# One step for the second batch's numerators, with its attention, the down products and the first output weights moved earlier

## The chip, the core and the metric

The kernel runs on one core of a Trainium2 chip. TensorE (PE) multiplies matrices, VectorE (DVE), ScalarE (ACT) and GpSimd (POOL) do elementwise work, and SyncE (SP) issues most DMA transfers. Each engine runs its instructions in the order in which the program gives them, and engines wait for each other by semaphores. The metric is the device time of one execution in microseconds (us). Before the change it is 306.09 us, the median of three runs (305.92 to 306.23).

## The reference

```
phi(x) = outer(S1 @ x, S2 @ x)            # 8 x 8 = 64 features for each token and head
kv  = sum over s of phi(k)[s] v[s]        # 64 x 32 for each batch and head
z   = sum over s of phi(k)[s]
x   = (phi(q) @ kv) / (phi(q) @ z + 1e-6) # the attention's output
x   = x as rows: 4352 tokens x 128        # 4 batches x 1088 tokens, 4 heads x 32
out = (silu(x @ w_gate) * (x @ w_val)) @ w_out   # 128 -> 1536 -> 128
```

The inputs are float64 in memory; the kernel reads them as pairs of 32-bit words. The attention needs all keys of a batch before the first output of that batch exists. The feed-forward part is three products of 4352 x 128 x 1536.

## The kernel before, in words

**Units and down products.** The tokens are cut into 12 blocks, three to a batch: two of 384 tokens and one of 320. The 1536 hidden columns are cut into 12 chunks of 128. `unit(i, j)` makes block i's chunk j: two PE products (gate and val, L773) into two PSUM banks, Silu of the gate on ACT (L779), and gate times val on DVE (L790) into one of 27 slots of `hbuf`. `down()` takes the first entry of `todo` and multiplies that chunk by `wo[:, j, :]`, adding into the block's bank (L804). After chunk 11, `store` transposes the block on DVE (L833) and SP writes it out (L839). The first six units are `late`: DVE is busy then, so ACT copies the val product and POOL multiplies later (`catch_up`, L796).

**Banks.** `bank()` hands out four PSUM banks in turn (g0, g1, g2, acc); once down products begin, `free_banks.pop()` takes `acc` out of the turn for the sums. Block 1's sum lies in g1, every other block's in acc (`down`).

**Weights.** The float64 weights arrive in pieces: gate and val in five (chunks 0, 1-2, 3-5, 6-8, 9-11), `wo` in four of three chunks each, `("wo", 0)` to `("wo", 3)`. `load_next` takes the next piece from the list `coming` and loads it into one of four raw buffers (L152). `narrow` turns a piece into float32 in three steps, each `part(name, i)` taking one: two DVE operations on the high words (L216, L217); two ACT operations (L221, L222); two DVE operations (L224, L230) and the final product (L239, on POOL but for the first val piece and half of each two-chunk piece, which DVE does), after which the next piece's load is issued. For the first val piece alone (`split`), the third step is cut in two, so that L224 is issued ahead of the first block's division results (L486) and the rest behind them.

**The loop around the change.** After a startup that mixes batch 0's attention, the first weight pieces and six late units, a loop runs over `seq`, 30 units of batch 0 numbered z = 0 to 29. z = 12 to 14 are block 0's chunks 6 to 8, z = 15 to 17 block 1's, z = 18 to 20 block 2's (320 tokens); z = 21 to 29 are chunks 9 to 11 in the same way. `parts` says after which unit a step of a later weight piece is issued: a piece's steps stand at z, z+1 and a little later. From z = 17 on each unit is followed by one `down()` (in the order block 0 chunk 0, 1, 2, ...) and by one step of `attentions()`. The rest of batch 0's down products follow the loop without units between them. Then batches 1 to 3 run as 36 units each, with a down product after each unit.

**The attention of batches 1 to 3** is the generator `attentions()`; each `yield` ends a step. For batch 1: transposes of k and q (L274, L509), key products and query sketches on PE (L301, L289), key features on DVE (L324), their sums on POOL (`feature_sums`, L494), key-value sums on PE (`values`, L335, L638), a copy and a transpose of them (`spread_out`, L648, L652) and six DMAs that spread them over the partitions (L658, L659). Then `query_step` on DVE: query features against the key sums (L679), reduction (L686), a reciprocal and a scaling (L695 to L701), features again (L324) and their transpose (L710). Last, `numerators` on PE (L730) and copies to `xT` (L747), from which batch 1's units read. Before, batch 1's query step and numerators run in two parts: the first three of nine column groups ahead of batch 1's first unit (up to the mark `"first"`), the other six while block 3 (batch 1's first) is worked on.

Of the kernel before, what the change touches and what calls it, by code (L numbers as in the profile page):

```python
# [18 lines left out]
def kernel(  # L19
# [28 lines left out]
    nc = tc.nc  # L48
    P = nc.NUM_PARTITIONS
# [6 lines left out]
    NC = (NX + 3) // 4  # L56
    F = R * R
    NCH = Dff // P
# [45 lines left out]
    wv = const.tile([P, NCH, P], FP32, name="wv")  # L104
# [6 lines left out]
    raw = {}  # L111
# [23 lines left out]
    coming = [(w, i) for i in range(len(pieces["wg"])) for w in ("wg", "wv")]  # L135
    coming += [("wo", i) for i in range(len(pieces["wo"]))]

    def load_next():
        if not coming:
            return  # L140
        name, i = coming.pop(0)
        dst, src = weights[name]
        c0, c1 = pieces[name][i]
        if name == "wo":
            part = src.rearrange("(c p) d -> p c d", p=P)[:, c0:c1, :]
        else:
            part = src.rearrange("p (c f) -> p c f", f=P)[:, c0:c1, :]
        if not wide_w:
            nc.sync.dma_start(out=dst[:, c0:c1, :], in_=part)
            return  # L150
        t = raw[name, i] = stage.tile([P, 3, P], I64, tag="raw", name="raw", bufs=NRAW)
        nc.sync.dma_start(out=t[:, 0 : c1 - c0, :], in_=part)  # L152
# [42 lines left out]
                ps[0:32, 0:w], warm[:, 0:32], warm[:, 0:w], start=True, stop=True  # L195
            )

    def narrow(dst, raw, shape, engine=nc.gpsimd, split=False):

        words = raw.bitcast(I32)
        pat = "p (n w) -> p n w" if len(shape) == 2 else "p c (n w) -> p c n w"
        words = words.rearrange(pat, w=2)
        lo = words[..., 0].bitcast(U32)
        hi = words[..., 1]
        first = len(shape) == 2  # L210
        tag = "s" if first else ""
        e, m = (
            stage.tile(shape, I32, tag=n + tag, name=n, bufs=6) for n in ("exp", "man")
        )
        f = m[:].bitcast(FP32)
        nc.vector.tensor_scalar(e[:], hi, 0x7FF00000, None, op0=ALU.bitwise_and)  # L216
        nc.vector.tensor_scalar(  # L217
            m[:], hi, 0xFFFFF, 0x100000, op0=ALU.bitwise_and, op1=ALU.bitwise_or
        )
        yield  # L220
        nc.scalar.activation(e[:], e[:], AF.Relu, bias=rebias[: shape[0], :], scale=8.0)  # L221
        nc.scalar.activation(f, m[:], AF.Copy, scale=2.0**-20)  # L222
        yield
        nc.vector.scalar_tensor_tensor(  # L224
            out=e[:], in0=hi, scalar=-(1 << 31), in1=e[:],
            op0=ALU.bitwise_and, op1=ALU.bitwise_or,
        )
        if split:
            yield
        nc.vector.scalar_tensor_tensor(  # L230
            out=f, in0=lo, scalar=2.0**-52, in1=f, op0=ALU.mult, op1=ALU.add
        )
        mul = nc.vector if first else engine
        p2 = e[:].bitcast(FP32)
        todo = [(mul, slice(None))]
        if shape[1] == 2:
            todo = [(nc.vector, slice(0, 1)), (mul, slice(1, 2))]
        for engine, c in todo:
            engine.tensor_tensor(out=dst[:, c], in0=f[:, c], in1=p2[:, c], op=ALU.mult)  # L239
        if not first:  # L240
            load_next()
        yield

    def narrow_w(name, i):
        c0, c1 = pieces[name][i]
        if wide_w:
            dst = weights[name][0]
            t = raw.pop((name, i))
            split = (name, i) == ("wv", 0)
            engine = nc.vector if split else nc.gpsimd  # L250
            yield from narrow(
                dst[:, c0:c1, :], t[:, 0 : c1 - c0, :], [P, c1 - c0, P], engine, split
            )

    def run(*gens):
        for g in gens:
# [200 lines left out]
    def divide(b, x0, n, nd, among=()):  # L457


        w = 32 * n  # L460
        t0 = S * b + 64 * x0
        dT = apool.tile([P, 2 * XS, 32], FP32, tag="dT", name="dT", bufs=2)
        rc = apool.tile([P, 2 * XS], FP32, tag="rc", name="rc", bufs=2)
        rd = apool.tile([P, 2 * XS, 32], FP32, tag="rd", name="rd", bufs=2)
        nc.vector.transpose(
            out=dT[:, 0 : 2 * n, :].rearrange("p (a x) t -> p a x t", a=2),
            in_=nd[1][:, :, 0:w].rearrange("p a (x t) -> p a x t", t=32),
        )
        for name in among[:1]:
            part(name, 0)  # L470
        nc.vector.tensor_scalar_add(rc[:, 0 : 2 * n], dT[:, 0 : 2 * n, 0], 1e-6)
        nc.vector.reciprocal(rc[:, 0 : 2 * n], rc[:, 0 : 2 * n])
        nc.vector.transpose(
            out=rd[:, 0 : 2 * n, :], in_=rc[:, 0 : 2 * n].unsqueeze(2).to_broadcast([P, 2 * n, 32])
        )
        for name in among[1:]:
            part(name, 0)
        xs = xT[:, t0 : t0 + 2 * w].rearrange("p (x a t) -> p a x t", a=2, t=32)
        rs = rd[:, 0 : 2 * n, :].rearrange("p (a x) t -> p a x t", a=2)
        flat, deep = "p (x t) -> p x t", "p a (x t) -> p a x t"  # L480
        if isinstance(nd[0], list):
            todo = [(xs[:, a], nd[0][a][:, 0:w].rearrange(flat, t=32), rs[:, a]) for a in (0, 1)]
        else:
            todo = [(xs, nd[0][:, :, 0:w].rearrange(deep, t=32), rs)]
        for x, num, r in todo:
            nc.vector.tensor_tensor(out=x, in0=num, in1=r, op=ALU.mult)  # L486
        for name in among[1:]:
            part(name, 0)
# [43 lines left out]
    def attentions():  # L532
# [15 lines left out]
        fac = None, qab  # L548
# [28 lines left out]
            (NC - 1, NC, kvz[:, 1, 0 : 2 * F], kvz[:, 1, 2 * F : 4 * F]),  # L577
        ])
        spread = spread_out(1, kvz[:, 0, :])
        for _ in range(4):  # L580
            yield
            run_copies(copies, 1)
        step = query_step(1, fac, spread)
        yield from step(0, 3)
        numerators(1, spread, 0, 3)
        yield "first"
        yield from step(3, NC)
        phk = hbuf[:, NH - 6 :, :].rearrange("p s (n h i j) -> p (s n) h i j", h=1, i=R, j=R)
        phk = phk.rearrange("p (c h) o i j -> p c (h o) i j", h=H)
        yield from features(phk, fac2, ())  # L590
        zs = feature_sums(phk)
        yield from turns(3)
        yield "pe"
        numerators(1, spread, 3, NC)
        kv = bank()
        values(kv, phk, zs)
        kp, qp = wide("a"), wide("b")
# [21 lines left out]
    def run_copies(copies, n):  # L619
        for f, *args in copies[:n]:  # L620
            f(*args)
        del copies[:n]
# [175 lines left out]
    def down():  # L798

        i, j = todo.pop(0)  # L800
        n = SPLIT if i == LAST else blocks[i][1]
        if j == 0:
            acc[i] = bank("g1" if i == 1 else "acc")
        nc.tensor.matmul(  # L804
            acc[i][:, 0:n],
            wo[:, j, :],
            hidden[i, j][:, 0:n],
            start=(j == 0),
            stop=(j == NCH - 1),
        )  # L810
        if i != LAST:
            hidden.pop((i, j))
            slots.append(slot_of[i, j])
        if j == NCH - 1:
            store(i, n)
# [34 lines left out]
    def part(name, i):  # L850

        next(fills[name, i], None)
# [96 lines left out]
    def parts_of(n):  # L949

        for _ in range(n):
            if ahead[0] not in ("pe", "end"):
                ahead[0] = next(att, "end")
# [34 lines left out]
    def both(i, *names):  # L988
        return [(name, i) for name in names]
# [1 line left out]
    w = ("wg", "wv")  # L991

    parts = {}
    for z, p in enumerate(both(3, *w) + both(4, *w) + [("wo", i) for i in range(4)]):
        z += z // 2 * 4
        for at in (z, z + 1, z + 2 + z % 6):
            parts.setdefault(at, []).append(p)
# [2 lines left out]
    seq += [(i, j) for j0 in (6, 9) for i in range(3) for j in range(j0, j0 + 3)]  # L1000
    order = [(i, j) for i in range(3) for j in range(NCH)]
    for z, (i, j) in enumerate(seq):
        if z == 17:
            free_banks.pop()
            turn[0] %= 4
        unit(i, j)
        for p in parts.get(z, ()):
            part(*p)
        if z in (24, 25, 26):
            catch_up()  # L1010
        if z == 6:
            load_k(1)
            load_v(1, [nc.sync] * 4)
            load_q(1)
        if z >= 17:
            todo.remove(order[0])
            todo.insert(0, order.pop(0))
            down()
        if z >= 17:
            parts_of(1)  # L1020
    todo.sort()
    while todo:
        for _ in range(min(3, len(todo))):
            down()
        if ahead[0] != "first":
            parts_of(1)
    while ahead[0] != "first":
        parts_of(1)

    slots[:] = range(NH - 6)  # L1030

# [2 lines left out]
    for b in range(1, B):  # L1034
        for z in range(3 * NCH):
            i, j = z // NCH, z % NCH
            if (b, z) in ((1, NCH), (2, 0), (2, 2 * NCH)):
                group()
            unit(3 * b + ((0, 2, 1)[i] if b == B - 1 else i), j)
            for _ in range(2):  # L1040
                if len(todo) > LAG:
                    down()
            parts_of(2 if b == 1 and z in (0, 4, 6, 7, 8) else 1)
    ps = wide("a")[:, 0, 0:D]
    for j in range(NCH):
        if todo and j % 4 == 0:
# [40 lines left out]
```

## Time and profile before

| what | value |
|---|---|
| median of the runs | 306.09 us (305.92 to 306.23) |
| the profiled execution: its own time | 306.09 us |
| its span in the trace | 304.4 us |
| PE busy | 297.9 us, 2186 matmul records |
| DVE busy | 170.0 us |
| ACT busy | 93.8 us |
| POOL busy | 37.8 us |
| granted PE clock | 1.00 throughout |

The time around the span is 306.09 - 304.4 = 1.7 us. A float32 product shows up as two matmul records. Ends of matmuls are modelled and overlap their successor, so the starts tell how long a product holds PE: in a run of 384-token products they are 0.645 us apart, in a run of 320-token products 0.54 us. A row of the timeline gives start, duration, engine, line and operation, then the tiles written and read; a bracket at its end gives the idle time of the engine before it and what ended that.

### The profile page before, as it was taken

Reading aid. Unit: us, or ns where it says so; the run is one execution under the profiler, and the core shown is the slowest. Engines: PE = TensorE matmul, PEld = TensorE weight load, DVE = VectorE, ACT = ScalarE, POOL = GpSimd, SP = SyncE. Lnnn points to the kernel's source line nnn. Section 1 sums busy time; section 2 is a strip of 40 time slices with the busy share of each in tenths; the row PEclk is TensorE's granted clock in tenths of the full one; section 3 lists DMA queues with packets and bytes.
Section 4 is the critical chain, followed back from the end, with each engine's and each line's share of the span. In section 5 each row is a group of like instructions: output and inputs, shape, how many; then the busy total and the mean of one; then the engine's idle time right before and its main releaser. Section 6 shows DMA issues by size and latency. Waiting matters only on the chain.

```text
span 304.4 us, 5416 instructions
## 1 busy us (share of the span) xinstructions
PE 297.9 (98%) x2186; PEld 190.4 (63%) x2186; DVE 170.0 (56%) x334; ACT 93.8 (31%) x219; POOL 37.8 (12%) x54
## 2 busy tenths in 40 slices
PE   8899999999999999999999999999999999999995
PEld 7545566657665557555676655555676556676664
DVE  3997988692636991788932478822323322333321
ACT  3566764422102222322222222222322222222230
POOL 3216222174000051070000000000000000000000
PEclk9999999999999999999999999999999999999999
DMA  7463390404511000400100200100100100100101
GB/s 197 139 201 106 103 313 12 149 14 146 117 28 22 0 2 20 110 0 0 26 3 2 49 0 2 26 0 0 22 6 0 22 3 0 26 0 2 21 0 26
DMA packets 26136, 14.57 MB, mean 48 GB/s; under 512 B 18688, under 2 KB 24192, under 8 KB 26112
## 3 DMA queue, kind: packets, MB, share of 16 engines
q1 hardware_dynamic: 25456, 14.13, 18.1%
q8 instruction: 17, 0.28, 0.3%
q10 hardware_dynamic: 656, 0.10, 0.2%
q14 instruction: 7, 0.06, 0.1%
HBM read 11.41 MB, written 2.23 MB: 45 GB/s over the span
## 4 chain that ended last, share of the span: by engine, by line
PE 95%; DVE 2%; DMA 2%; issue 0%; ACT 0%; SPq 0%
PE bank L773 58%; PE bank L804 28%; DMA kld<-in_k_dram 2%; PE a L730 1%; PE b L289 1%; PE bank L335 1%; PE a L819 1%; PE a L301 1%; PE bank L348 0%; PE bank L301 0%; PE a L392 0%; PE a L444 0%; PE a L335 0%; PE b L301 0%; PE b L730 0%
## 5 line engine op out<-in xcount | busy, mean ns | idle before, releaser
L790 DVE TENSOR_TENSOR hbuf<-sg,bank 128x384 f32<-128x384 f32 (+1 forms) x138 | 72.9, 529 | 99.3 <-PE bank L773 97.6
L779 ACT ACTIVATE sg<-bank 128x384 f32<-128x384 f32 (+1 forms) x144 | 68.0, 473 | 163.0 <-PE bank L773 159.8
L773 PE MATMUL bank<-xT,wg 128*128 128x384 f32 (+1 forms) x288 | 112.5, 472 | 0.0
L773 PE MATMUL bank<-xT,wv 128*128 128x384 f32 (+1 forms) x288 | 111.5, 469 | 0.2 <-DVE wv L239 0.2
L804 PE MATMUL bank<-hbuf,wo 128*128 128x384 f32 (+2 forms) x288 | 105.1, 460 | 0.0
L773 PEld LDWEIGHTS bank<-xT,wv 128*128 128x128 f32 x288 | 54.5, 190 | 33.7 <-DVE hbuf L790 0.9
L804 PEld LDWEIGHTS bank<-hbuf,wo 128*128 128x128 f32 x288 | 54.5, 190 | 32.0
L773 PEld LDWEIGHTS bank<-xT,wg 128*128 128x128 f32 x288 | 53.7, 190 | 32.3 <-issue 1.6
L494 POOL TENSOR_TENSOR zs<-hbuf 128x1024 f32<-128x1024 f32 x2 | 4.7, 2360 | 51.5 <-DVE hbuf L324 37.6
L833 DVE STREAM_TRANSPOSE o<-bank 128x384 f32<-128x384 f32 (+2 forms) x12 | 6.6, 549 | 7.8 <-PE bank L804 7.5
L679 DVE TENSOR_TENSOR phq<-spread,qab 128x768 f32<-128x768 f32 x9 | 9.7, 1076 | 0.5 <-DMA spread<-spread 0.5
L221 ACT ACTIVATE exp<-exp,rebias 128x384 int32<-128x384 int32 (+3 forms) x15 | 8.3, 551 | 2.3 <-DVE exp L216 1.7
L710 DVE STREAM_TRANSPOSE phT<-phq 128x768 f32<-128x768 f32 x9 | 8.7, 968 | 0.1
L686 DVE TENSOR_REDUCE dot<-phq 128x96 f32<-128x768 f32 x9 | 8.5, 947 | 0.1
L324 DVE TENSOR_TENSOR phq<-qab 128x768 f32<-128x768 f32 x9 | 8.5, 942 | 0.0
L747 ACT COPY xT<-a 128x64 f32<-128x64 f32 (+3 forms) x7 | 2.3, 367 | 18.2 <-PE b L730 11.8
L224 DVE SCALAR_TENSOR_TENSOR exp<-raw,exp 128x384 int32<-128x384 int32 (+2 forms) x14 | 7.0, 503 | 0.0
L230 DVE SCALAR_TENSOR_TENSOR man<-raw,man 128x384 f32<-128x384 uint32 (+2 forms) x14 | 6.9, 492 | 0.0
L222 ACT ACTIVATE man<-man 128x384 f32<-128x384 int32 (+3 forms) x15 | 6.8, 452 | 0.0
L494 POOL TENSOR_TENSOR zs<-zs 128x512 f32<-128x512 f32 (+1 forms) x6 | 6.6, 1100 | 0.5
L239 POOL TENSOR_TENSOR wg<-man,exp 128x384 f32<-128x384 f32 (+1 forms) x5 | 4.0, 801 | 18.2 <-DVE man L230 14.0
L274 DVE STREAM_TRANSPOSE kT<-kld 128x384 f32<-128x384 f32 (+2 forms) x9 | 5.9, 690 | 0.6 <-DMA kld<-in_k_dram 0.6
(127 smaller groups left out, 161.4 us busy)
## 6 DMA issues: line engine op xcount, KB each, us to landing
kld<-in_k_dram SPq DMA_DIRECT2D x4, 544.0 KB, 4.6
vld<-in_v_dram SPq DMA_DIRECT2D x12, 144.0 KB, 5.3
qld<-in_q_dram SPq DMA_DIRECT2D x3, 544.0 KB, 4.4
raw<-in_moe_w_out_dram SPq DMA_DIRECT2D x4, 384.0 KB, 4.5
out_dram<-o SPq DMA_DIRECT2D x28, 48.0 KB, 1.8
raw<-in_moe_w_gate_dram SPq DMA_DIRECT2D x3, 384.0 KB, 3.4
raw<-in_moe_w_val_dram SPq DMA_DIRECT2D x3, 384.0 KB, 3.7
out_dram<-o SPq DMA_DIRECT2D x16, 40.0 KB, 1.7
```

What stands on the lines that cost most here:

```text
L221: nc.scalar.activation(e[:], e[:], AF.Relu, bias=rebias[: shape[0], :], scale=8.0)
L224: nc.vector.scalar_tensor_tensor(out=e[:], in0=hi, scalar=-(1 << 31), in1=e[:], op0=ALU.bitwise_and, op1=ALU.bitwise_or,)
L230: nc.vector.scalar_tensor_tensor(out=f, in0=lo, scalar=2.0**-52, in1=f, op0=ALU.mult, op1=ALU.add)
L324: engine.tensor_tensor(out=phk[:, c0:c1, :, :, :].rearrange("p c h i j -> p (c h) i j"), in0=ka.unsqueeze(3).to_broadcast([P, n, R, R]), i ...
L494: add = lambda o, a, b: nc.gpsimd.tensor_tensor(out=o, in0=a, in1=b, op=ALU.add)
L679: nc.vector.tensor_tensor(out=phq[:, c0:c1, :, :, :], in0=zrep.unsqueeze(1).to_broadcast([P, n, H, R, R]), in1=f.unsqueeze(3).to_broadcast ...
L686: nc.vector.tensor_reduce(out=dot[:, x, :], in_=phq[:, c0:c1, :, :, :].rearrange("p c h j i -> p (c h) j i"), axis=AX.X, op=ALU.add,)
L710: nc.vector.transpose(out=phT[:, :, :, c0:c1, :].rearrange("p h g c t -> p c (h g) t"), in_=phq[:, c0:c1, :, :, :].rearrange("p c h (g i) ...
L773: nc.tensor.matmul(o[:, 0:n], w[:, j, :], xT[:, t0 : t0 + n], start=True, stop=True)
L779: nc.scalar.activation(sg[:, 0:n], g[:, 0:n], AF.Silu)
L790: nc.vector.tensor_tensor(out=hj[:, 0:n], in0=sg[:, 0:n], in1=u[:, 0:n], op=ALU.mult)
L804: nc.tensor.matmul(acc[i][:, 0:n], wo[:, j, :], hidden[i, j][:, 0:n], start=(j == 0), stop=(j == NCH - 1),)
```

## The change

It does six things. The query step and the numerators of batch 1 are done in one piece of nine column groups, ahead of batch 1's first unit. The attention generator is advanced from z = 13 on instead of 17. Down products follow the units from z = 14 instead of 17 (up to z = 25, and one after z = 29), the bank `acc` leaves the turn at z = 14, and the load of batch 1's k, v and q is asked for after z = 5 instead of 6. After the loop the numerators are issued when four down products are left. The load and the narrowing of `("wo", 0)` move ahead of the last gate and val pieces. The cut in the first val piece's third step goes away, so that its L224 comes behind the division results.

```diff
     coming = [(w, i) for i in range(len(pieces["wg"])) for w in ("wg", "wv")]
     coming += [("wo", i) for i in range(len(pieces["wo"]))]
+    coming.remove(("wo", 0))
+    coming.insert(-5, ("wo", 0))
...
-        if split:
-            yield
         nc.vector.scalar_tensor_tensor(
             out=f, in0=lo, scalar=2.0**-52, in1=f, op0=ALU.mult, op1=ALU.add
         )
...
-        for name in among[1:]:
-            part(name, 0)
         xs = xT[:, t0 : t0 + 2 * w].rearrange("p (x a t) -> p a x t", a=2, t=32)
...
-        for _ in range(4):
+        for _ in range(2):
             yield
-            run_copies(copies, 1)
-        step = query_step(1, fac, spread)
-        yield from step(0, 3)
-        numerators(1, spread, 0, 3)
+            run_copies(copies, 2)
+        yield from query_step(1, fac, spread)(0, NC)
         yield "first"
-        yield from step(3, NC)
+        numerators(1, spread, 0, NC)
+        yield
...
         yield "pe"
-        numerators(1, spread, 3, NC)
         kv = bank()
...
-    for z, p in enumerate(both(3, *w) + both(4, *w) + [("wo", i) for i in range(4)]):
+    late = both(3, *w) + [("wo", 0)] + both(4, *w) + [("wo", i) for i in range(1, 4)]
+    for z, p in enumerate(late):
         z += z // 2 * 4
         for at in (z, z + 1, z + 2 + z % 6):
             parts.setdefault(at, []).append(p)
...
-        if z == 17:
+        if z == 14:
             free_banks.pop()
             turn[0] %= 4
         unit(i, j)
         for p in parts.get(z, ()):
             part(*p)
         if z in (24, 25, 26):
             catch_up()
-        if z == 6:
+        if z == 5:
             load_k(1)
             load_v(1, [nc.sync] * 4)
             load_q(1)
-        if z >= 17:
+        if 14 <= z < 14 + NCH or z == len(seq) - 1:
             todo.remove(order[0])
             todo.insert(0, order.pop(0))
             down()
-        if z >= 17:
+        if z >= 13:
             parts_of(1)
     todo.sort()
     while todo:
-        for _ in range(min(3, len(todo))):
+        for _ in range(min(3, len(todo) - 4)):
             down()
-        if ahead[0] != "first":
-            parts_of(1)
+        for _ in range(2):
+            if ahead[0] != "first":
+                parts_of(1)
+        if len(todo) == 4:
+            break
     while ahead[0] != "first":
         parts_of(1)
+    parts_of(1)
+    while todo:
+        down()
...
-            parts_of(2 if b == 1 and z in (0, 4, 6, 7, 8) else 1)
+            parts_of(1)
```

The narrowing steps therefore stand as follows (loop index z after whose unit each of the three steps is issued):

| piece | before | after |
|---|---|---|
| wo 0 | 12, 13, 14 | 6, 7, 8 |
| wg 4, wv 4 | 6, 7, 8 and 7, 8, 10 | 7, 8, 10 and 12, 13, 14 |
| wo 1 | 13, 14, 16 | 13, 14, 16 |
| wo 2 | 18, 19, 20 | 18, 19, 20 |
| wo 3 | 19, 20, 22 | 19, 20, 22 |

| first down product that reads the piece | before | after |
|---|---|---|
| wo 0 (chunk 0) | z = 17 | z = 14 |
| wo 1 (chunk 3) | z = 20 | z = 17 |
| wo 2 (chunk 6) | z = 23 | z = 20 |
| wo 3 (chunk 9) | z = 26 | z = 23 |

More of the change, by code (lines that the diff above doesn't have):

```diff
@@ L196, in keep_warm, with narrow @@
             )
-    def narrow(dst, raw, shape, engine=nc.gpsimd, split=False):
+    def narrow(dst, raw, shape, engine=nc.gpsimd):
         words = raw.bitcast(I32)
@@ L248, in narrow_w @@
             t = raw.pop((name, i))
[L249 to L253, printed above, removed]
+            engine = nc.vector if (name, i) == ("wv", 0) else nc.gpsimd
+            yield from narrow(dst[:, c0:c1, :], t[:, 0 : c1 - c0, :], [P, c1 - c0, P], engine)
     def run(*gens):
```

## The prediction

> **What bounds the kernel now.** I read the page's busy shares and clock first, then PE's waits, then the timelines of PE, DVE and POOL from 44 to 120 us.
>
> ```profile
> PE 297.9 (98%) x2186; PEld 190.4 (63%) x2186; DVE 170.0 (56%) x334; ACT 93.8 (31%) x219; POOL 37.8 (12%) x54
> ...
> PEclk9999999999999999999999999999999999999999
> ```
> ```profile
> engine line waited for: us in total, times, longest us
> PE bank L194 <- PEq L1071: 0.9, 1, 0.9
> ...
> PE bank L773 <- DVE wv L239: 0.2, 1, 0.2
> ```
>
> PE is the bound. It is full at full clock; its waits are short and lie in the startup, and from 27 us on product follows product. So the change can gain only what it takes off PE, and loses whatever makes PE stand still. The rows I price with:
>
> ```profile
> 53.86 0.70 PE L773 MATMUL bank<-xT,wv 128*128 128x320 f32 x2
> ...
> 72.66 0.29 PE L289 MATMUL a<-s,qT 128*32 128x64 f32 x8
> ...
> 90.00 2.96 PE L804 MATMUL bank<-hbuf,wo 128*128 128x320 f32 x10
> ...
> 116.07 1.21 PE L335 MATMUL bank<-hbuf,vld 128*32 128x64 f32 x72
> ...
> 164.69 1.21 PE L335 MATMUL bank<-hbuf,vld 128*32 128x64 f32 x72
> ```
> ```profile
> 54.67 0.49 DVE L790 TENSOR_TENSOR hbuf<-sg,bank 128x320 f32<-128x320 f32 x1
> 55.07 0.55 DVE L224 SCALAR_TENSOR_TENSOR exp<-raw,exp 128x384 int32<-128x384 int32 x1
> 55.54 0.55 DVE L230 SCALAR_TENSOR_TENSOR man<-raw,man 128x384 f32<-128x384 uint32 x1
> ...
> 78.77 0.96 DVE L679 TENSOR_TENSOR phq<-spread,qab 128x768 f32<-128x768 f32 x1 [0.50 <-DMA spread<-spread]
> ```
> ```profile
> 56.17 1.00 POOL L239 TENSOR_TENSOR wo<-man,exp 128x384 f32<-128x384 f32 x1 [5.39 <-DVE man L230]
> ```
>
> The reader is to see wo 2's last step: unit z = 20 starts its val product at 53.86, DVE multiplies it 0.81 later, then come L224, L230 and POOL's product, and the weights are ready at 57.17, 3.31 us after 53.86. Today the first down product that reads them starts at 62.74, so nobody notices.
>
> **The change part by part.** Times are on before's clock; products hold PE 0.645 us (384) or 0.54 (320).
>
> *Numerators, a gain.* The first part fills the time between the down products (a run from 77.50; 12 x 0.645 + 7 x 0.54 later it is 89.02) and the next down product at 90.00: 0.98. The second lies between a down product of 114.15 (+ 0.645) and the value sums at 116.07: 1.27. One full set, batch 2's, lies between a down product of 162.56 (+ 0.54) and 164.69: 1.59. So 2.25 become 1.59: **-0.66**. The small DVE operations of the query step also become fewer, hidden behind PE.
>
> *The bitwise sum, a loss.* L224 of the first val piece runs at 14.44, before the division product at 14.74, which waits for PE's product of 14.09 + 0.56. It lies in DVE idle time today. Behind it, it lengthens a DVE chain without gaps up to the val weights that end PE's wait at 19.02. Its price is the spacing L224 to L230 of that size (13.10 to 13.27): **+0.17**. Ends: 0 (some gap absorbs it) and 0.28 (a whole operation).
>
> *Loads.* The wo 0 load takes the slot of 23.52 in SP's queue, the last gate and val pieces slide one slot each to 26.18 and 33.33. They land within 6.2 us (the longest landing of such a piece), by 32.4 and 39.5, for first steps that run after 37 and at 43.5. Batch 1's k is issued at about 35.7, as now, and lands within 6.1, by 41.8; its transpose now runs at 45.4. q, by 38.13 + 7.0 = 45.1, is read at 48.6. v, four transfers from 36.24, is read at 67.7. Cost 0; each us that k came later than 45.4 would hold unit 14's product behind it on DVE. No more is issued than before. Attention's ACT copies lie in ACT's gaps of 1.44 us per unit, at cost 0.
>
> *wo 1, a wait.* Units 14 to 16, now with a down product each, start 1.94 us apart: 44.07, 46.01, 47.94. Unit 17 starts at 49.88, its down product (chunk 3, from wo 1) is due at 51.17. Unit 16's val product starts at 48.59, DVE multiplies at +0.91 = 49.50, L224 at 49.98, L230 at 50.45, POOL 0.63 later, 51.08 to 52.08. POOL to PE is not timed before; the nearest row is DVE to PE, 0.15 (val weights end 18.87, PE 19.02). PE resumes at 52.23: **+1.07**. Ends 0.9 and 1.3 (half to a whole L224 of delay either way).
>
> *wo 2, a wait.* From 52.23: key products and sketches follow as today 0.74 and 2.34 later, unit 18 at 55.31, unit 20's val product at 59.39, its down product (chunk 6, from wo 2) due at 59.93. Unit 20's DVE product could start at 59.39 + 0.81 = 60.20, but key features are queued before it (unit 18's product 56.76, two weight operations 0.27 each, features 2 x 0.60, unit 19's 58.90, the same with one feature operation) and it starts at 60.44. L224 0.40 later, L230 another 0.47, POOL another 0.63, 1.00 of product, 0.15: PE resumes at 63.09. **+3.15**. Ends 2.9 (DVE free) and 3.5. Behind the waiting down product stands everything on PE; ACT and DVE then wait for PE.
>
> The Trainium skill ("TensorE: Matmul & The Clock Gate", Part 1) says that a PE left idle for a whole window of about 3.4 us falls to half clock, until it has been busy for about such a window. That speaks against this change, since the wait above comes near it. No idle stretch in this trace is above 0.9 us and no slice shows less than full clock, so no row here tests it. By the page the sum would be an estimated 1.7 us more (half of 3.4); I leave it out.
>
> wo 3 is not late: on POOL it now follows the feature sums (from 62.9; 5.3 us as 64.91 to 70.23 before) and its own L230 at 68.2, is ready at 69.8, and its reader is due at 72.7. The feature sums themselves end 68.2; their reader (L638) is due at 68.7. Thin: each us late there is a us on PE.
>
> *The query step among the units, a wait.* From 63.09 PE runs a down product (0.645) and units 21 and 22 with one each (1.94 apiece), then the value sums 0.09 later at 67.7; the last sketches start 3.38 after these (69.28 to 72.66 before) at 71.07, unit 23's val product at 72.03 and unit 25's at 75.91. From last sketches to L679 it takes 78.77 - 72.66 = 6.11 us (copy, transpose, six DMAs issued one after another), so L679 starts at 77.18. Before, nothing urgent was queued behind it. Now unit 25's DVE product is, due at 76.82 and run at 78.05. Then DVE alternates: product 0.47 or 0.40, store transpose 0.51, L679 or L686 0.87 (spacings at 85.44 to 85.95 and 97.14 to 98.47). Unit 26 gets 79.90, 27 81.24, 28 82.51, 29 83.78. Units from 26 on have no down products between them, so three banks run out: block 1's sum takes g1, which unit 29's val product (30 units after z = 14 on a turn of three) has just filled. It must wait for DVE: 83.78 + 0.49 + 0.13 = 84.40, against 81.73 if nothing waited: **+2.67**. Ends 0.8 (only the delay of unit 25) and 3.6 (another DVE operation of 0.95 in the way).
>
> After that DVE has 12 us of down products for its remaining 7 us of query step, and the numerators find their input ready; block 3 starts 2.2 us after them, more than the 0.6 us of copies.
>
> **Sum**: -0.66 + 0.17 + 1.07 + 3.15 + 2.67 = +6.40. The profiled execution took 306.09 us (span 304.4, 1.7 around it), the same as the median: 312.5.
>
> **Rivals.**
> 1. *Only the weights stall.* The banks or an earlier spread hide the last wait: 306.09 + 3.73 = 309.8. For: DVE idles for 3.9 and 1.2 us near this place before. Against: L679 is tied to the sketches on PE, whatever else moves.
> 2. *The attention is later still*: a queue or sum that I hold for thinly covered (feature sums 0.5 us, spread DMAs) slips, and PE restarts slowly after standing still. Bounded by one more spread of 1.9 us (a transfer's landing): 314.4.
> 3. *The other side: the weights are in time.* If PE doesn't wait for wo 1 and wo 2 (their POOL products done by 51.0 and 59.8, over 3 us sooner than I work out), DVE's backlog must also vanish; then only the gain and the bitwise sum are left, 305.6. Against: the instruction order has wo 2's last step behind unit 20's DVE product, and PE's product behind that on a wait for POOL; both are dependences of data.
> 4. *The change does less than it says*: the numerators are still two sets in effect. The order shows one set of 32 products on PE, so no weight.
>
> **How the numbers follow.** My forecast 0.67, rival 1 0.17, rival 2 0.11, rival 3 0.05. The time is the forecast's, 312.5. Its own ends: the low ends sum to -0.66 + 0 + 0.9 + 2.9 + 0.8 = 3.9, the high ends to -0.66 + 0.28 + 1.3 + 3.5 + 3.6 = 8.0; not all fall on one side, so about 311 to 314. The range that leaves 2 in 10 out takes in rival 1 and most of rival 2: 309.5 to 314.3. About 0.2% (0.6 us) is what a measurement can tell from no change. Slower has the first three cases, 0.95; rival 3 at -0.5 lies about on the border: same 0.03, faster 0.02.
>
> **What would show it.** PE's waits list two of L804 on POOL's wo product, about 1.1 and 3.1 us, and gate products (L773) and one L804 on DVE's L790, some 2.7 us in all. L730 stands in one block of about 1.6 us ahead of batch 1. PE busy falls by about 0.7 us or, if ends are modelled into a wait, somewhat differently. The forecast is wrong if no wait of L804 on POOL above 0.5 us appears, or if the clock falls after the long one, or if DVE's L790 of unit 25 isn't held behind L679.

## The result and the profile after

| | before | after |
|---|---|---|
| median of the runs | 306.00 us (305.84 to 306.23, 4 runs) | 313.55 us (313.42 to 314.80, 4 runs) |
| ratio to before, 95% interval | | 1.0255 [1.0228, 1.0282] |
| profiled execution, its span | 306.09, 304.4 us | 313.42, 311.7 us |
| mean granted PE clock | 1.00 | 0.995 |

The changed kernel is slower by 7.55 us by the medians; 312.5 was forecast, within 309.5 to 314.3. The lines of the changed kernel's file have moved: gate and val products are L767 (L773 before), down products L798 (L804), DVE's unit product L784 (L790), the last product of a weight piece L240 (L239), its two DVE operations L227 and L231 (L224 and L230), key-value sums L333 and L632 (L335 and L638), sketches L287 (L289), the query step L673 and L680 (L679 and L686), numerators L724 (L730).

From the page of the changed kernel, busy time by engine and the granted clock in 40 slices of 7.8 us:

```profile
PE 300.2 (96%) x2122; PEld 190.0 (61%) x2122; DVE 169.2 (54%) x328; ACT 93.8 (30%) x218; POOL 37.8 (12%) x54
...
PEclk9999999979999999999999999999999999999999
```

PE has 64 matmul records fewer and yet 2.3 us more of busy time: a part of its work took longer. The ninth slice (62 to 70 us) shows why, its clock is not full. PE's waits in the changed kernel, largest first:

```profile
engine line waited for: us in total, times, longest us
PE bank L798 <- POOL wo L240: 3.7, 2, 2.9
PE bank L798 <- DVE hbuf L784: 1.3, 1, 1.3
PE bank L197 <- PEq L1072: 0.9, 1, 0.9
PE bank L767 <- DVE hbuf L784: 0.4, 1, 0.4
```

Three of the four rows are new; only PE's own start (L197) was there before. Where they lie, from the timeline of PE (start, duration, line, tiles; in brackets the idle time before and what ended it):

```profile
50.39 0.81 PE L767 MATMUL bank<-xT,wv 128*128 128x384 f32 x2
52.00 0.91 PE L798 MATMUL bank<-hbuf,wo 128*128 128x384 f32 x2 [0.79 <-POOL wo L240]
...
59.27 0.70 PE L767 MATMUL bank<-xT,wv 128*128 128x320 f32 x2
62.85 0.94 PE L798 MATMUL bank<-hbuf,wo 128*128 128x384 f32 x2 [2.89 <-POOL wo L240]
63.60 1.48 PE L767 MATMUL bank<-xT,wg 128*128 128x384 f32 x2
64.87 1.49 PE L767 MATMUL bank<-xT,wv 128*128 128x384 f32 x2
66.15 1.24 PE L798 MATMUL bank<-hbuf,wo 128*128 128x384 f32 x2
67.23 0.81 PE L767 MATMUL bank<-xT,wg 128*128 128x384 f32 x2
...
83.91 0.70 PE L767 MATMUL bank<-xT,wv 128*128 128x320 f32 x2
85.89 12.29 PE L798 MATMUL bank<-hbuf,wo 128*128 128x384 f32 x40 [1.27 <-DVE hbuf L784]
```

Read the starts. The down product of 52.00 was due at 50.39 + 0.645 = 51.04, and the one of 62.85 at 59.27 + 0.54 = 59.81: PE loses 0.96 and 3.04 us to wo 1 and wo 2. After the second, four products that should take 4 x 0.645 = 2.58 us take 67.23 - 62.85 = 4.38, and their durations reach 1.49 where 0.81 is usual. The windows of that stretch (window; busy us and count of PE, PEld, DVE, ACT, POOL; granted clock; DMA share; GB/s) name the cause:

```profile
62.60:64.60 2.00, 1.74 (x4) 1.15 (x5) 0.47 (x1) 0.00 (x0) 2.00 (x2) 0.75 0.24 52
64.60:66.60 2.00, 2.00 (x4) 1.01 (x3) 0.13 (x1) 0.49 (x1) 1.84 (x3) 0.50 0.63 226
66.60:68.60 2.00, 2.00 (x7) 1.14 (x6) 1.77 (x3) 0.47 (x1) 1.38 (x2) 0.90 0.03 8
```

The clock goes to one half at 63.6 us, 0.75 us after PE has resumed, and stays there until 67.0. What is late at the other two places, from the timeline of DVE:

```profile
60.31 0.48 DVE L784 TENSOR_TENSOR hbuf<-sg,bank 128x320 f32<-128x320 f32 x1
60.70 0.55 DVE L227 SCALAR_TENSOR_TENSOR exp<-raw,exp 128x384 int32<-128x384 int32 x1
61.17 0.55 DVE L231 SCALAR_TENSOR_TENSOR man<-raw,man 128x384 f32<-128x384 uint32 x1
...
78.74 0.96 DVE L673 TENSOR_TENSOR phq<-spread,qab 128x768 f32<-128x768 f32 x1 [1.73 <-DMA spread<-spread]
79.61 0.55 DVE L784 TENSOR_TENSOR hbuf<-sg,bank 128x384 f32<-128x384 f32 x1
...
85.26 0.48 DVE L784 TENSOR_TENSOR hbuf<-sg,bank 128x320 f32<-128x320 f32 x1
```

and of POOL:

```profile
61.80 1.00 POOL L240 TENSOR_TENSOR wo<-man,exp 128x384 f32<-128x384 f32 x1 [9.86 <-DVE man L231]
```

The chain of wo 2 is unit 20's product (60.31), two DVE operations, POOL's product until 62.80, PE 0.05 later. Further on DVE stands idle for 1.73 us in front of the query step's first instruction, which waits for the spread's DMAs, with unit 25's product behind it until 79.61; unit 29's product, which PE's down product of 85.89 waits for, ends at 85.74.

### The profile page after: what moved, and what is told of

It is laid out like the page before. It is cut to its first block, busy times and chain, and to the rows that moved or that the text cites. A ratio compares the mean times of both kernels' runs of the same rounds, so it can differ in the third digit from the quotient of the medians.

```text
span 311.7 us, 5283 instructions
## 1 busy us (share of the span) xinstructions
PE 300.2 (96%) x2122; PEld 190.0 (61%) x2122; DVE 169.2 (54%) x328; ACT 93.8 (30%) x218; POOL 37.8 (12%) x54
## 4 chain that ended last, share of the span: by engine, by line
PE 90%; DVE 5%; DMA 1%; issue 1%; POOL 1%; ACT 0%; SPq 0%; DVEq 0%
PE bank L767 54%; PE bank L798 27%; DMA kld<-in_k_dram 1%; PE a L724 1%; DVE hbuf L784 1%; PE b L287 1%; PE bank L333 1%; PE a L813 1%; PE a L299 1%; POOL wo L240 1%; DVE man L231 1%; DVE exp L227 1%; PE bank L346 0%; PE bank L299 0%; PE a L390 0%
## 5 line engine op out<-in xcount | busy, mean ns | idle before, releaser
L784 DVE TENSOR_TENSOR hbuf<-sg,bank 128x384 f32<-128x384 f32 (+1 forms) x138 | 72.9, 529 | 108.9 <-PE bank L767 108.5
L773 ACT ACTIVATE sg<-bank 128x384 f32<-128x384 f32 (+1 forms) x144 | 68.0, 473 | 166.8 <-PE bank L767 164.4
L767 PE MATMUL bank<-xT,wg 128*128 128x384 f32 (+1 forms) x288 | 113.3, 475 | 0.6 <-DVE hbuf L784 0.4
L767 PE MATMUL bank<-xT,wv 128*128 128x384 f32 (+1 forms) x288 | 112.2, 471 | 0.2 <-DVE wv L240 0.2
L798 PE MATMUL bank<-hbuf,wo 128*128 128x384 f32 (+2 forms) x288 | 105.8, 462 | 5.0 <-POOL wo L240 3.7
L798 PEld LDWEIGHTS bank<-hbuf,wo 128*128 128x128 f32 x288 | 54.6, 191 | 38.8 <-POOL wo L240 4.8
L767 PEld LDWEIGHTS bank<-xT,wv 128*128 128x128 f32 x288 | 54.7, 191 | 34.2 <-issue 1.0
L767 PEld LDWEIGHTS bank<-xT,wg 128*128 128x128 f32 x288 | 53.8, 191 | 33.6 <-DVE hbuf L784 2.0
L673 DVE TENSOR_TENSOR phq<-spread,qab 128x768 f32<-128x768 f32 x9 | 9.7, 1075 | 1.7 <-DMA spread<-spread 1.7
L224 ACT ACTIVATE exp<-exp,rebias 128x384 int32<-128x384 int32 (+3 forms) x15 | 8.3, 551 | 2.3 <-DVE exp L219 1.7
L680 DVE TENSOR_REDUCE dot<-phq 128x96 f32<-128x768 f32 x9 | 8.5, 942 | 0.0
L741 ACT COPY xT<-a 128x512 f32<-128x512 f32 (+1 forms) x6 | 2.1, 402 | 19.6 <-PE a L724 19.6
L227 DVE SCALAR_TENSOR_TENSOR exp<-raw,exp 128x384 int32<-128x384 int32 (+2 forms) x14 | 7.1, 505 | 0.0
L231 DVE SCALAR_TENSOR_TENSOR man<-raw,man 128x384 f32<-128x384 uint32 (+2 forms) x14 | 6.9, 493 | 0.0
L240 POOL TENSOR_TENSOR wo<-man,exp 128x384 f32<-128x384 f32 x4 | 4.0, 998 | 18.4 <-DVE man L231 18.4
L741 DVE COPY xT<-b 128x512 f32<-128x512 f32 x3 | 2.1, 691 | 7.5 <-PE a L724 7.5
```

The lines of the kernel that those rows point to most:

```text
L227: nc.vector.scalar_tensor_tensor(out=e[:], in0=hi, scalar=-(1 << 31), in1=e[:], op0=ALU.bitwise_and, op1=ALU.bitwise_or,)
L231: nc.vector.scalar_tensor_tensor(out=f, in0=lo, scalar=2.0**-52, in1=f, op0=ALU.mult, op1=ALU.add)
L673: nc.vector.tensor_tensor(out=phq[:, c0:c1, :, :, :], in0=zrep.unsqueeze(1).to_broadcast([P, n, H, R, R]), in1=f.unsqueeze(3).to_broadcast ...
L680: nc.vector.tensor_reduce(out=dot[:, x, :], in_=phq[:, c0:c1, :, :, :].rearrange("p c h j i -> p (c h) j i"), axis=AX.X, op=ALU.add,)
L767: nc.tensor.matmul(o[:, 0:n], w[:, j, :], xT[:, t0 : t0 + n], start=True, stop=True)
L773: nc.scalar.activation(sg[:, 0:n], g[:, 0:n], AF.Silu)
```

## The experiments

Twelve kernels ran. A ratio is to the kernel before on the same chip, with its 95% interval. The theory: the loss is the sum of the two weight waits, the clock after the second, and the query step's wait on DVE. The rivals put parts of it elsewhere. Eight of them correct one thing or more in the changed kernel, four start from the kernel before.

**1. Work for PE in the long wait.** Is it the clock that makes four products cost 1.8 us too much, or does POOL's feature sum or the loads beside them do it?

```diff
+    fill = {20: 12}
     for z, (i, j) in enumerate(seq):
...
+            if z in fill:
+                keep_warm(fill[z])
             down()
```

> The changed kernel with 12 extra bf16 products (512 columns, into the next unit's bank, results unused) on PE ahead of the down product of z = 20, the one that waited 2.89 us for wo 2. Theory (the long idle stretch lets the granted clock fall): at an estimated 0.21 us each the products fill some 2.5 of the 2.9 us without moving the end of the wait, the clock stays at 1.00, and the 1.8 us that units 21 and 22 lost at half clock come back: 311.7 us. Rival (the clock falls for another reason, such as the end of a burst of loads or the mix of work): the clock dips again at the same place, 313.4 us or a little more.

311.90 us, 1.0195 [1.0167, 1.0223], 1.65 less than the changed kernel, with 12 products more. Its PE timeline at the same place:

```profile
59.88 2.78 PE L197 MATMUL bank<-const-bfloat16-1.0 128*32 128x512 bf16 x12
62.84 0.91 PE L798 MATMUL bank<-hbuf,wo 128*128 128x384 f32 x2 [0.18 <-POOL wo L240]
63.59 0.81 PE L767 MATMUL bank<-xT,wg 128*128 128x384 f32 x2
64.23 0.81 PE L767 MATMUL bank<-xT,wv 128*128 128x384 f32 x2
```

The wait ends at the same time (62.84 beside 62.85), POOL and the loads work beside it as before, and the next products are 0.81 long and 0.64 apart. So it is the clock. The first product after the wait takes 0.75 instead of 0.645 here too; that 0.10 is not the clock's, which leaves 1.70 of the 1.80 to it.

**2. Less work in the wait.** How much idle time is too much?

```diff
+    fill = {20: 5}
```

> The changed kernel with 5 extra bf16 products on PE ahead of z = 20's down product instead of 12 (the 12 took 2.6 us): about 1.1 us of the 2.9 are filled, 1.8 us of idle time remain. Theory (the clock falls after a stretch of little work, and half again as much work in it is enough to keep it): the clock stays at 1.00 and the time is that of the 12, 311.9 us. Rival (an idle stretch of 1.8 us is enough): the clock falls again and 313.5 us result.

311.67 us, 1.0182 [1.0146, 1.0218]. PE's timeline:

```profile
59.91 1.26 PE L197 MATMUL bank<-const-bfloat16-1.0 128*32 128x512 bf16 x5
62.87 0.91 PE L798 MATMUL bank<-hbuf,wo 128*128 128x384 f32 x2 [1.70 <-POOL wo L240]
63.62 0.81 PE L767 MATMUL bank<-xT,wg 128*128 128x384 f32 x2
```

1.26 us of products at the start of the gap were enough in both executions of this kernel (mean granted clock 0.998 and 1.000); 1.70 us of idle time behind them leave the clock at 1.00.

**3. The output weights sooner.** wo 1 and wo 2 are loaded and narrowed ahead of the last gate and val pieces, all pieces closer together.

```diff
+    tail = [("wo", 0), ("wo", 1), ("wo", 2), ("wg", 4), ("wv", 4), ("wo", 3)]
+    coming = [p for p in coming if p not in tail] + tail
...
+    late = both(3, *w) + [("wo", i) for i in range(3)] + both(4, *w) + [("wo", 3)]
     for z, p in enumerate(late):
-        z += z // 2 * 4
-        for at in (z, z + 1, z + 2 + z % 6):
+        z += z // 2 * 3
+        for at in (z, z + 1, z + 2 + z % 5):
```

> The changed kernel with wo 0, wo 1 and wo 2 loaded and narrowed ahead of the last gate and val pieces (third steps at z = 7, 9 and 12, the last gate and val at 14 and 17, wo 3 at 19). Theory (two waits for weights, and the clock that falls in the second): no down product waits for POOL's wo product, and 0.96 + 3.04 + 1.80 = 5.8 us come back: 307.7 us, perhaps 0.3 more if the feature sums are then just late. Rival (DVE is overfull with attention work among the units and the waits only show where it comes out): PE's waits move to DVE's unit products or features, and 311 us or more remain.

309.25 us, 1.0111 [1.0081, 1.0141]: 4.3 us come back, 1.55 less than expected. Its PE waits:

```profile
engine line waited for: us in total, times, longest us
PE bank L798 <- DVE hbuf L784: 1.8, 2, 1.3
PE bank L197 <- PEq L1072: 0.9, 1, 0.9
PE a L632 <- POOL zs L490: 0.6, 1, 0.6
```

No wait on POOL's wo product is left, and the clock is full in every slice. But the row of L798 on DVE now counts two: besides the known 1.27, the first down product waits 0.52 us, the feature sums are 0.56 late (L632), and units 10 to 12 lose 0.26. These 1.3 us are the rival's: five pieces narrowed in fewer units crowd DVE. The traced execution is the slowest of the four (310.75 us, the others 309.10 to 309.27); nearly all of the difference lies in the startup, where the first block's division product stands at 15.20 us instead of 13.76.

**4. Only wo 2, one unit sooner.**

```diff
+        z -= p == ("wo", 2)
-        for at in (z, z + 1, z + 2 + z % 6):
+        for at in (z, z + 1, z + 2 + z % 6 % 5):
```

> The changed kernel with wo 2's three narrowing steps one unit sooner (z = 17, 18, 19). Theory: the wait of z = 20's down product shrinks by one unit (1.72 us), from 2.9 to about 1.2 us, which is too short for the clock to fall: 3.5 us come back, 309.9 us. If an idle stretch of about 1.2 us is enough for the clock to fall, only 1.7 come back: 311.7 us. If the wait is DVE's backlog and not the step's place, nothing comes back: 313.4 us.

310.56 us, 1.0142 [1.0122, 1.0161], 0.66 above what was expected. The wait shrinks from 2.89 to 0.99 (PE resumes at 61.02), the clock stays up, and 0.49 us appear at L632: with PE sooner there, the thin cover of the feature sums is gone. One unit sooner brought 3.0 us, more than the 1.9 us of the wait itself.

**5. Block 1's sum in another bank.** In g2 instead of g1, so that it doesn't need the bank of unit 29's val product.

```diff
-            acc[i] = bank("g1" if i == 1 else "acc")
+            acc[i] = bank("g2" if i == 1 else "acc")
```

> The changed kernel with block 1's sum in bank g2 (filled by unit 28's val product) instead of g1 (filled by unit 29's). Theory (the first down product of block 1 waits for DVE to empty g1): it waits for unit 28's DVE product, 1.27 us sooner, and that much comes back: 312.2 us; the shorter bank waits of units 27 to 29 stay. Rival (DVE's query step limits the numerators anyway): the numerators then wait instead, 313.4 us.

312.02 us, 1.0173 [1.0138, 1.0209]. Its PE timeline:

```profile
84.18 0.70 PE L767 MATMUL bank<-xT,wv 128*128 128x320 f32 x2
84.89 12.28 PE L798 MATMUL bank<-hbuf,wo 128*128 128x384 f32 x40
```

The down products follow with no wait; the 1.27 us was the bank.

**6. The query step one step later**, so that unit 25's product stands ahead of the query step's first instruction on DVE.

```diff
             run_copies(copies, 2)
+        yield
         yield from query_step(1, fac, spread)(0, NC)
```

> The changed kernel with one more empty step ahead of batch 1's query step, so that its first operation (the one that waits for the six spread transfers) stands behind unit 25's DVE product and not in front of it. Theory (the waiting operation holds up unit 25's product, and every bank behind it): unit 25's product runs on time, the bank waits of units 27 to 29 (0.4 us and more) shrink, the first down product of block 1 still waits for unit 29's product; 1.1 us come back: 312.4 us. Rival (the spread transfers set DVE's whole chain, whatever stands in front): nothing comes back, 313.4 us.

312.34 us, 1.0204 [1.0182, 1.0227]. Unit 25's product runs at 78.11 and the query step behind it from 79.19; units 26 to 29 lose no time to a bank, and only the wait for g1 stays, 1.27 us. So holding unit 25's product behind the transfer cost about the 1.2 us that came back (the medians of this run and of the changed kernel).

**7. Both 5 and 6.**

> The changed kernel with both edits: block 1's sum in g2, and the query step one unit later. Theory: nearly all of the 2.60 us between unit 26 and the first down product of block 1 come back, 311.0 us, and DVE still has its query step done before the numerators. Rival (the numerators then wait for DVE): 311.8 us or more, with a wait of L724 for DVE's L704.

311.15 us, 1.0159 [1.0125, 1.0193]: 2.4 us back. From unit 26's gate product to the down products it now takes 83.63 - 78.84 = 4.79 us, with products of 1.29 + 3 x 1.08 = 4.53 in it.

The four executions of this kernel took 311.11, 309.30, 311.19 and 312.41 us, at mean granted clocks of 0.994, 1.000, 0.994 and 0.994. One of the four of run 5 stands out in the same way: 310.43 us at 0.998, the others 311.88 to 312.39 at 0.992 to 0.995. In these two the clock seems not to have fallen, though the kernel is the same; they were not traced.

**8. Both places at once**: 3, 5 and 6 together. Are the two losses independent?

> The changed kernel with both corrections at once: the output weights sooner (as in the run with wo 1 and wo 2 loaded and narrowed ahead of the last gate and val pieces) and the query step's wait undone (block 1's sum in bank g2, the query step one part later). If the two places are independent, the gains add: 313.5 - 4.3 - 2.4 = 306.8 us, that is level with the kernel before or 0.3% above it, and the waits left are the small ones of the crowded vector queue (0.5, 0.6 and 0.3 us). Rival, the places are tied: sooner weights move the last sketches and the query step sooner too, the banks run out elsewhere, and less than 1.5 us of the second gain is left: 307.7 us or more.

307.22 us, 1.0032 [1.0019, 1.0044]. From 3 to here the ratio falls by 0.0079, 2.4 us, and the median by 2.0; 2.4 were expected, and the rival needed less than 1.5. They are independent, as far as 0.4 us can tell. The waits left, from its PE waits:

```profile
PE a L633 <- POOL zs L490: 0.6, 1, 0.6
PE bank L799 <- DVE hbuf L785: 0.5, 1, 0.5
```

They are the two that the crowded DVE made in 3, and 1.1 us of them is about what still separates this kernel from the one before.

**9. The numerators alone.** The kernel before, with the query step and the numerators in one piece and four down products left for them; the attention stays at z = 17.

```diff
...
-        step = query_step(1, fac, spread)
-        yield from step(0, 3)
-        numerators(1, spread, 0, 3)
+        yield from query_step(1, fac, spread)(0, NC)
         yield "first"
-        yield from step(3, NC)
+        numerators(1, spread, 0, NC)
...
-        for _ in range(min(3, len(todo))):
+        for _ in range(min(3, len(todo) - 4)):
             down()
...
```

> The kernel before with the numerators of batch 1 in one step and four down products left, with nothing else moved: the attention still starts at z = 17. Theory (the early attention is what the single set needs, since DVE needs some 14 us from the spread transfers to the last transpose): L730 waits for L710, about 2.5 us less what other waits take, and 307.5 us result. Rival (the early start wasn't needed): no wait, 305.4 us.

309.57 us, 1.0115 [1.009, 1.014]. In its trace, the largest of PE's waits:

```profile
PE a L728 <- DVE phT L708: 3.3, 1, 3.3
```

And the two windows behind it, with the columns of the windows above:

```profile
92.00:96.00 4.00, 3.47 (x68) 2.24 (x69) 1.08 (x2) 0.70 (x2) 0.00 (x0) 0.74 0.00 0
96.00:100.00 4.00, 4.00 (x13) 2.47 (x12) 1.03 (x3) 0.49 (x1) 0.00 (x0) 0.83 0.07 10
```

The whole query step is too long for DVE from there, so the merged numerators (L728 in this file) find their input late by 3.28 us. The clock falls a second time at another place, after another producer: (0.26 + 0.17) x 4 = 1.7 us of clock are missing. The expectation had left that out again. Batch 2's sketches (L289), 1.66 us long on PE before (118.52 to 120.18), take 1.14 here (122.40 to 123.54).

**10. The attention from z = 15, before's down products.** As 9, with the attention two units sooner and wo 3's third step one unit later; the output weights and their readers stay.

```diff
-        if z >= 17:
+        if z >= 15:
             parts_of(1)
```

> The kernel before with the numerators of batch 1 in one step, four down products left behind them, the attention advanced from z = 15, and wo 3's last narrowing step one unit later; the down products still begin at z = 17, the weights keep their order and the bitwise sum stays cut. Theory (one set of numerators instead of two is the only gain in the change, 0.66 us, and its waits come from the rest): no wait on PE above 0.5 us, 305.4 us (0.2% faster than before). Rival (with the query step whole ahead of batch 1, DVE is always late somewhere): a wait of 1 us or more appears on PE and the time is 306.5 us or more.

306.30 us, 1.0008 [0.9992, 1.0023]: no difference from before, where 305.4 was expected. The twelve executions fall apart: five took 305.3 to 305.8 us, about the forecast, and seven 306.3 to 307.3. The traced one took 305.48, so its trace does not show what made the others longer. In it the numerators still wait 0.29 us for DVE, and wo 3's two operations now run beside POOL's feature sums. From the timeline of DVE in this kernel:

```profile
63.15 1.61 DVE L224 SCALAR_TENSOR_TENSOR exp<-raw,exp 128x384 int32<-128x384 int32 x1
64.68 1.08 DVE L230 SCALAR_TENSOR_TENSOR man<-raw,man 128x384 f32<-128x384 uint32 x1
```

and from that of POOL:

```profile
63.07 2.27 POOL L494 TENSOR_TENSOR zs<-zs 128x512 f32<-128x512 f32 x2
65.42 0.93 POOL L494 TENSOR_TENSOR zs<-zs,phk 128x256 f32<-128x256 f32 x1
```

The two took 0.55 each before.

**11. Three down products left.** As 10, with three left and wo 3's third step one more unit later, behind the feature sums.

```diff
-        for at in (z, z + 1, z + 2 + z % 6):
+        for at in (z, z + 1, z + 2 + z % 6 + 2 * (z == 19)):
...
-        for _ in range(min(3, len(todo))):
+        for _ in range(min(3, len(todo) - 3)):
```

> The kernel before with the numerators of batch 1 in one step and the attention from z = 15, as in the run with four down products left, but with three left, and with wo 3's last narrowing step after z = 24, behind the feature sums on POOL. Theory (the two waits of that run, 0.3 us for the feature sums, whose POOL operations ran beside wo 3's L224 and both took longer, and 0.3 us for the last L708, ate the gain of 0.66 us): both waits go, 305.3 us or 0.2% faster than before. Rival (the waits move): a wait of L745's copies on the first gate product of batch 1, or of a down product on wo 3, and 306 us.

305.02 us (12 runs) beside 305.86 for the kernel before on that chip, 0.9967 [0.9948, 0.9985]. This one beats both kernels, the one before by 0.8 us. Its PE waits:

```profile
engine line waited for: us in total, times, longest us
PE bank L194 <- PEq L1075: 0.9, 1, 0.9
PE bank L444 <- ACT kvz L932: 0.4, 1, 0.4
...
PE bank L771 <- DVE wv L239: 0.2, 1, 0.2
```

Nothing is left but the waits of the startup. The one-step numerators are worth having where nothing is paid for them.

**12. The bitwise sum alone.** The kernel before without the cut in the first val piece's third step.

```diff
-            split = (name, i) == ("wv", 0)
+            split = False
...
-        for name in among[1:]:
-            part(name, 0)
```

> The kernel before, with nothing changed but the bitwise sum of the first val piece, which now comes behind the division results as in the changed kernel. Theory: it lengthens a DVE chain without gaps up to the val weights of the second unit by one spacing, 0.17 us: 306.2 us. Rival (PE's earlier gate product or a gap takes it up): 306.0 us. The difference is near what five rounds can tell; the trace's distance from the division's PE product to the second unit's val product (4.93 us before) shows it otherwise.

306.23 us, 1.0004 [0.9992, 1.0017]. The time cannot tell 0.17 us from nothing; the trace can. From the division product to the val product that waits for the weights it takes 19.22 - 14.10 = 5.12 us, 19.02 - 14.09 = 4.93 before: +0.19.

## Why the prediction was right, and which term was mis-sized

The direction, the places and most of the sizes were right. One step failed: the forecast named the clock's fall behind the long wait among the signs of being wrong and put its price at nothing, and the clock fell. That the total still came within 1.1 us is in part luck, since two things outside the sum, +1.80 and -0.85, go against each other. By its own terms, measured in the changed kernel's trace:

| term | forecast | measured |
|---|---|---|
| numerators in one set | -0.66 | -0.58 |
| bitwise sum | +0.17 | +0.21 |
| wait for wo 1 | +1.07 | +0.96 |
| wait for wo 2 | +3.15 | +3.04 |
| clock after it | left out | +1.80 |
| query step's wait | +2.67 | +2.60 |
| not in the sum: a pause at the second sketches, an earlier start | 0 | -0.85 |
| sum | +6.40 | +7.18 |

The two spans differ by 311.7 - 304.4 = 7.3.

- *Numerators.* The set that is left holds PE from 97.93 (where the down products from 85.89 on end) to 99.60, 1.67 us against 0.98 for the small part before (+0.69), and the 1.27 of the second part are gone: -0.58. Run 11 shows that a gain of this kind reaches the end where nothing else waits.
- *Bitwise sum.* 18.90 - 13.76 = 5.14 us from the division product to the val product against 4.93, and 0.19 by itself in run 12. Shown as a spacing in the trace; too small for the time.
- *wo 1 and wo 2.* The chains ran as worked out: unit, L227, L231, POOL, PE. Both waits came out about 0.1 us short, since POOL's product released PE after 0.05 us, where the forecast took DVE's 0.15. Run 3 takes both waits away, run 4 shortens the second, and the time follows.
- *The clock.* This is the mis-sized term: the forecast said that "no row here tests it" and left it out. It measured 1.80 us, 1.70 of them given back by run 1. The Trainium skill ("TensorE: Matmul & The Clock Gate", Part 1) gives a whole idle window of about 3.4 us as the condition and as long a busy time for the recovery; the forecast's estimate from it, 1.7, was the size. The half clock lasted 3.4 us here (63.6 to 67.0), which agrees: the three windows lack (0.25 + 0.50 + 0.10) x 2 = 1.70 us of clock. The condition does not agree: 2.89 us of idle time were enough (3.04 between the time due and the start) in all four executions of the changed kernel (mean clock 0.995 in each), and the measurement decides.
- *The query step.* From the last sketches (72.63) to L673 (78.74) it took 6.11 us, the forecast's figure. Unit 25's product was held as said, DVE alternated as said, and the down product of g1 started at 85.89 instead of 78.76 + 1.29 + 3 x 1.08 = 83.29. Runs 5 and 6 part it in two, some 1.2 to 1.5 us for the bank and some 1.2 for the held product. Run 7 has 0.26 us left with no wait for DVE, so about a tenth of the 2.60 is not DVE's.
- *Loads, wo 3, feature sums.* No wait for them shows. The feature sums ended at 68.05 and their reader came at 70.29, which the half clock had moved back: in run 1, without it, the reader came at 68.58, still with no wait. In run 4 PE came 1.8 us sooner once more, and the sums were 0.49 late. The cover, some 0.5 us, was as thin as the forecast held it to be.
- *Not in the sum.* Before, PE paused for about 0.5 us at the second batch's sketches, between the two rows that follow (0.22 of it idle time that no releaser explains); the changed kernel, in the third row, doesn't:

```profile
118.52 1.09 PE L289 MATMUL b<-s,qT 128*32 128x64 f32 x60
119.83 0.42 PE L289 MATMUL b<-s,qT 128*32 128x64 f32 x12 [0.22 <-issue]
```
```profile
126.33 1.21 PE L287 MATMUL b<-s,qT 128*32 128x64 f32 x72
```

The pause goes with the numerators in two parts: it is gone in run 9, which starts from the kernel before and changes them, and it is there in run 12 (1.57 us to the next product), which leaves them. So by these rows the single set took some 0.5 us off PE beyond the term above; what makes PE pause is not known. And batch 0's division product came at 13.76 instead of 14.09. That differs between executions and isn't of the change: it is 14.10 in run 12, and between 13.66 and 15.20 in runs 1 to 8, whose code up to there is the changed kernel's. Together the two took back 0.85 us.

The rivals: the banks did run out (against 1), PE's slow restart that rival 2 named as a part of it was real though the spread didn't slip, and the weights were late (against 3).

## What to carry to other kernels

Moving a consumer sooner pays only if its producers move too: for each piece, set the end of its last step beside the start of its first reader before moving either. An instruction that waits for a transfer holds everything behind it in its engine's queue, and the buffers that those instructions would free, so place it behind the urgent work. Where PE waits about 3 us at a stretch, as here, count nearly 5, and where it can't be avoided, a little work for PE in it takes the clock's part away.

## What the runs showed of the hardware

- **The clock.** It fell after idle stretches of 2.88 to 2.89 us (the changed kernel and runs 5 to 7, which keep that wait) and 3.28 us (run 9). By the mean clocks it fell in 14 of the 16 executions with the first of these waits, and in two, one each of runs 5 and 7, it seems not to have. It didn't fall after 0.79, 0.99, 1.27 and, behind 1.26 us of products, 1.70 us. Nor does the fall come at a fixed time after PE's return: the clock is at one half from 63.6 us in the changed kernel (return at 62.85), from 93.95 in run 9 (return at 92.53), and in run 6 from 62.3, when PE was still idle (return at 62.88); each time it stays there for about 3.4 us. Where a limit lies between 1.70 and 2.88 us, if there is a fixed one, and whether it moves with the time at which the gap begins, stays open.
- **DVE beside POOL.** In run 10 a DVE operation of 0.55 us took 1.61 and another 1.08 while POOL summed, and POOL's own operations grew from 2.08 to 2.27 and from 0.73 to 0.93 (before's figures first). The Trainium skill ("SBUF — State Buffer", Who interferes with whom) says that a DVE instruction with two inputs in SBUF contends with a GpSimd instruction that reads SBUF. These rows agree. In run 11, which moved the two operations to the end of the sums, L224 was back at 0.55 us, while L230, beside the last sum, still took 1.09 and that sum 0.99. No run separates this effect's share of the time.
